# First-batch attention weights turned by TensorE, second-stage scores as one float32 product, and a new order of the work

## The chip, the cores and the metric

One NeuronCore of a Trainium2 chip runs the whole kernel. The metric is the device time of one execution in microseconds (us); each kernel has a median of several runs. The engines are named as the profile names them: PE is TensorE (PEld its weight loads), DVE is VectorE, ACT is ScalarE, POOL is GpSimd, and SP is the engine that issues nearly all DMAs.

## The reference, cut to what matters

Two stages, for 8 batches of 576 positions. The first is attention with a threshold over 8 heads of width 64; the second is a mixture of 4 causal attention experts of width 64, of which each position uses two.

```python
scores = q @ k.T / 8                                  # (8, 8, 576, 576)
thresh = max(scores, -1) - tau
attn = softmax(where(scores >= thresh, scores, -1e9))
x = merge_heads(attn @ v)                             # (8, 576, 512)
logits = x @ w_gate                                   # two of four experts, softmax over the two
for e in range(4):
    a = softmax(causal((x @ wq[e]) @ (x @ wk[e]).T / 8))
    out += gate[e] * (a @ (x @ wv[e]) @ wo[e])        # (8, 576, 512)
```

All inputs and outputs are float32.

## The kernel before

**First stage.** The heads are taken in pairs: a batch has 4 pairs, so there are 32, numbered n. `prep` (L868) loads k, q and v of a pair, turns k and q on PE by products with an identity (L638, shown as L1253) and copies the result to `kx` and `qx` on ACT. The queries of a pair come in tiles of 128; the 64 left over of two pairs share a fifth tile, which the odd pair handles: 9 tiles for two pairs, 18 for a batch. `scores` (L921) does a tile for both heads: four float32 products; two DVE reductions (`copied_min`, L722) that copy the scores from PSUM to a buffer `pp` and keep the minimum of the negated scores; a POOL operation that adds tau; on ACT the threshold (`kinked`, L741) and the exponential with its sum (L737). The weights are then divided by their sum and split into two float16 parts, a high part by POOL (L691) and the rest by DVE (L714), both in `hl` (L949, L950). `turned` (L963) has one DMA transpose on SP's queue put the tile's 18 blocks of 128x128 into `T`. `attnv` (L971) multiplies them with v, which `values_in` (L843) has also split in two float16 parts, after finding its largest value (a DVE reduction, two tiny products with ones, a reciprocal): 5 blocks x 3 terms x 2 heads = 30 products. ACT and DVE write the result as a rounded part and a rest in `x`.

**Second stage.** `moe` (L1193) follows each batch's fourth pair. For each of two expert pairs `projected` (L1015) makes q and k: 12 products for each half of the columns, ACT copies the rounded part from PSUM, and DVE subtracts it to leave the rest (`minus`, L676, shown as L674), so `q2` holds two parts. `scores2` (L1099) makes the scores in three terms (high x high, high x rest, rest x high); then come a masked minimum on DVE (L720), the exponential on ACT, the gate on POOL, `transp2` (turning on PE, copies on ACT, `blocks_out` L953), `attnv2` (float32 products) and `output`.

**Order.** No engine order is written out. Each operation gets a planned cost in ns and a place: the pair's number plus a value of its unit from the table `PLACE` plus one of its engine and output from `PLACE_OP`. `arrange` (L298) runs the whole program through a list schedule with these as priorities, and the order that comes out is each engine's. Even pairs and odd pairs have two sets of places (prefix none or `o`); `attnv2` borrows those of the first stage one to three pairs later (`AV2_AT`). A planned DMA transpose takes 3300 ns of SP and lands after 7000 (`TURN`). `fill` (L488) puts dummy products with `still` (L1250) in PE's long gaps of the first 160 us, so that PE keeps working.

Of the kernel before, what the change touches and what calls it, by code (L numbers as in the profile page):

```python
# [29 lines left out]
TURN = 3300, 7000  # L30
PLACE = {
# [27 lines left out]
    "ot40": 1.234288, "otload": -2.15, "ovload": 6.842465, "ovx": -0.4765129, "ovy": 0.19182, "perm": 3.2453,  # L59
# [4 lines left out]
}  # L64
PLACE_OP = {
    "ACT gw": -56.45884, "ACT kx": 19.09358, "ACT lg": -1.697393, "ACT p2": -0.2764889, "ACT pp": 7.008259,
    "ACT pt2": -3.430901, "ACT q2": 61.64586, "ACT q2d0": -19.44223, "ACT q2d1": -62.4638, "ACT qi": -6.081787,
    "ACT qx": -40.40309, "ACT qz0": -45.39163, "ACT qz1": -1.596204, "ACT tau_t": -6.23236, "ACT tq": -4.485027,
    "ACT v2": -31.44942, "ACT warm": -2.488699, "ACT wkh": -18.97201, "ACT woh": -17.61192, "ACT wqh": -32.6847,
    "ACT wvh": -29.69152, "ACT x": -20.71576, "ACT z0": 6.489924, "ACT z1": 39.36308, "ACT zt": 44.04483,  # L70
    "DVE col": -0.501858, "DVE gate": -41.56914, "DVE gt": -13.63018, "DVE gw": -58.71909, "DVE hl": 0.2197733,
    "DVE lg": -0.01591195, "DVE p2": 0.1799851, "DVE pp": 0.07334633, "DVE q2": 11.57007, "DVE qsc": -9.096009,
    "DVE st": 51.91258, "DVE still": 14.04606, "DVE tau_p": -1.901486, "DVE v2": -1.374655, "DVE vh": -18.09807,
    "DVE warm": -35.69132, "DVE x": -0.4135823, "DVE z0": 2.44509, "DVE z1": 25.41215, "DVE zt": 30.31674,
    "POOL col": -9.007673, "POOL hl": 23.92377, "POOL ident": -28.71514, "POOL mask": 29.11687,
    "POOL mask2": 1.757008, "POOL ones": 0.3521134, "POOL p2": -39.45817, "POOL q2d0": 16.35419,
    "POOL q2d1": -49.53155, "POOL qz0": -10.19174, "POOL qz1": -15.39161, "POOL st": -7.958867, "POOL tie": 30.51963,
    "POOL vh": -26.85869, "POOL vz0": -7.771182, "POOL vz1": -17.71229, "POOL wkl": -19.05416, "POOL wol": 14.28486,
    "POOL wql": 38.65369, "POOL wvh": -23.34791, "POOL wvl": -33.78734, "SP T": -0.2487632, "SP ki": -5.091671,
    "SP lg": -2.212828, "SP out": -56.49631, "SP qi": 6.936229, "SP st": -49.13195, "SP tk": 7.588376,  # L80
    "SP tq": -17.13129, "SP vz0": -2.828946, "SP vz1": 1.694837,
}
# [460 lines left out]
def kernel(  # L543
# [58 lines left out]
    for name, n in SLOTS.items():  # L602
        family(name, words[name], n)
# [680 lines left out]
```

## Time and profile before

| what | us |
|---|---|
| median of 3 runs | 849.94 |
| lowest and highest run | 848.79, 850.33 |
| profiled execution, its own time | 849.39 |
| profiled execution, span from first to last instruction | 847.6 |

The profile's page gives each engine's busy time as a share of the span: PE 92%, PEld 76%, DVE 89%, ACT 80%, POOL 52%. Busy time of PE is modelled, because products overlap in the array, so a busy PE is not one at its peak. The mean granted clock of TensorE is 0.977 of full speed.

### The profile page before, as it was taken

How to read it: one execution, taken by the hardware profiler on the slowest of the kernel's cores; microseconds unless marked ns; L12 is line 12 of the kernel's file. 1: busy time of each engine (PE TensorE's matmuls, PEld its weight loads, DVE VectorE, ACT ScalarE, POOL GpSimd, SP SyncE). 2: the span in 40 equal slices, each digit the busy share in tenths (PEclk: the TensorE clock that was granted, in tenths of full speed). 3: DMA queues.
4: the chain of work that ended last, by engine and by line, in shares of the span. 5: the costliest groups of instructions: out<-in, count | busy, mean ns of one | idle time of the engine just before them, and what ended most of it. 6: DMA issues, size and time to landing. Idle time of an engine off the chain costs nothing.

```text
span 847.6 us, 27874 instructions
## 1 busy us (share of the span) xinstructions
PE 776.1 (92%) x10836; PEld 641.6 (76%) x10836; DVE 752.4 (89%) x2149; ACT 678.5 (80%) x1784; POOL 444.6 (52%) x642
## 2 busy tenths in 40 slices
PE   8989898989999899989999899988999989998898
PEld 5767687767877687767977678776887769776797
DVE  3999989999899889999899998998989998999575
ACT  4887769988689876998689886898869986799464
POOL 5786535566256553566356653565625655366211
PEclk9999999999999899999999999998999999999999
DMA  7999985899758998799956989589966879557602
GB/s 159 187 182 188 184 161 112 161 178 189 141 112 167 156 190 157 109 176 177 177 124 134 189 157 180 110 166 167 179 149 105 168 153 187 140 109 117 135 13 76
DMA packets 442820, 127.65 MB, mean 151 GB/s; under 512 B 429504, under 2 KB 437952, under 8 KB 442688
## 3 DMA queue, kind: packets, MB, share of 16 engines
q1 hardware_dynamic: 440960, 125.48, 78.6%
q8 instruction: 85, 1.39, 0.7%
q10 hardware_dynamic: 1728, 0.39, 0.3%
q14 instruction: 47, 0.39, 0.2%
HBM read 31.47 MB, written 9.44 MB: 48 GB/s over the span
## 4 chain that ended last, share of the span: by engine, by line
DVE 40%; PE 37%; issue 8%; ACT 7%; DMA 5%; POOL 3%; ACTq 0%; SPq 0%; POOLq 0%; DVEq 0%
PE banks L629 33%; DVE hl L714 14%; DVE pp L725 11%; DMA T<-hl 4%; DVE p L720 3%; DVE x L714 2%; DVE vh L714 2%; PE banks L1253 2%; POOL hl L691 2%; DVE col L691 2%; ACT pp L743 2%; DVE col L699 1%; ACT pp L737 1%; ACT p L737 1%; PE banks L1250 1%
## 5 line engine op out<-in xcount | busy, mean ns | idle before, releaser
L691 POOL TENSOR_SCALAR hl<-pp,col 128x576 f16<-128x576 f32 x288 | 233.8, 819 | 138.2 <-DVE col L703 50.7
L714 DVE SCALAR_TENSOR_TENSOR hl<-pp,col,hl 128x576 f16<-128x576 f32 x288 | 269.4, 947 | 18.7 <-POOL hl L691 17.0
L743 ACT ACTIVATE pp<-pp,col 128x576 f32<-128x576 f32 x288 | 212.1, 778 | 29.9 <-POOL col L691 29.1
L725 DVE TENSOR_SCALAR_CACHE_REDUCE pp<-banks 128x576 f32<-128x576 f32 x288 | 211.2, 746 | 12.7 <-PE banks L629 12.5
L737 ACT ACTIVATE pp<-pp 128x576 f32<-128x576 f32 x288 | 194.9, 682 | 0.3
L629 PE MATMUL banks<-kx,qx 64*128 64x288 f32 x1024 | 169.2, 435 | 9.5 <-DVE pp L725 5.6
L629 PE MATMUL banks<-T,vh 128*64 128x128 f16 (+1 forms) x4800 | 145.7, 223 | 21.4 <-DVE pp L725 16.2
L629 PEld LDWEIGHTS <-vh 128*64 128x64 f16 x4800 | 135.2, 116 | 38.6 <-issue 36.6
L691 POOL TENSOR_SCALAR col<-col,tau_p 128x2 f32<-128x2 f32 x144 | 64.6, 449 | 168.7 <-DVE pp L725 76.3
L629 PEld LDWEIGHTS banks<-kx,qx 64*128 64x128 f32 x1024 | 101.1, 192 | 41.1 <-DVE pp L725 12.0
L737 ACT ACTIVATE p<-p,col 128x512 f32<-128x512 f32 (+3 forms) x135 | 79.4, 592 | 51.9 <-DVE col L720 51.2
L691 POOL TENSOR_SCALAR p<-p,col,gw 128x512 f32<-128x512 f32 (+3 forms) x115 | 85.2, 748 | 61.8 <-DVE col L703 45.1
L629 PE MATMUL banks<-wvh,x 128*128 128x260 f32 x320 | 65.3, 289 | 6.9 <-DVE x L714 5.2
L720 DVE CUSTOM_DVE_ANT_0 p<-banks,mask 128x512 f32<-128x512 f32 (+3 forms) x135 | 66.5, 513 | 1.2 <-PE banks L629 1.0
L629 PEld LDWEIGHTS banks<-wvh,x 128*128 128x128 f32 x320 | 51.8, 188 | 9.3 <-DVE x L714 6.4
L663 ACT ACTIVATE pt<-banks 128x384 f32<-128x384 f32 (+2 forms) x128 | 56.5, 511 | 2.6 <-PE banks L1253 1.7
L737 ACT ACTIVATION_READ_ACCUMULATOR pp<-pp 128x1 f32 x288 | 57.4, 199 | 0.0
L629 PE MATMUL banks<-pt,v 128*64 128x128 f32 (+1 forms) x960 | 52.4, 260 | 4.1 <-ACT pt L663 4.1
L714 DVE SCALAR_TENSOR_TENSOR x<-banks,col,x 128x256 fp32r<-128x256 f32 (+1 forms) x96 | 37.3, 407 | 20.1 <-ACT x L661 19.2
L629 PE MATMUL banks<-q,q 64*128 64x256 f32 (+3 forms) x384 | 50.2, 354 | 4.8 <-DVE pp L725 4.1
L629 PE MATMUL banks<-x,wqh 128*128 128x288 f32 x256 | 53.3, 300 | 0.0
L629 PE MATMUL banks<-x,wkh 128*128 128x288 f32 x256 | 53.1, 300 | 0.0
(121 smaller groups left out, 1403.3 us busy)
## 6 DMA issues: line engine op xcount, KB each, us to landing
ki<-in_k_dram SPq DMA_DIRECT2D x32, 256.0 KB, 3.7
vz<-in_v_dram SPq DMA_DIRECT2D x32, 256.0 KB, 3.2
qi<-in_q_dram SPq DMA_DIRECT2D x62, 128.0 KB, 3.1
out_dram<-st SPq DMA_DIRECT2D x29, 256.0 KB, 2.3
T<-hl SPq DMA_TRANSPOSE x144, 5.1
tk<-in_k_dram SPq DMA_DIRECT2D x16, 128.0 KB, 3.4
out_dram<-st SPq DMA_DIRECT2D x10, 128.0 KB, 2.4
vz<-in_v_dram SPq DMA_DIRECT2D x64, 16.0 KB, 2.7
```

Source lines behind the costliest of these rows:

```text
L629: lambda o, x, y: nc.tensor.matmul(o, x, y, start=start, stop=stop))
L663: run(e, t, [dst], [src], lambda d, s: nc.scalar.activation(d, s, AF.Copy))
L691: return m.tensor_scalar(d, s, x_, y_, op0=op0, op1=op1)
L699: lambda d, s: nc.vector.tensor_reduce(d, s, axis=axis, op=op, **({"negate": True} if negate else {}), **({"apply_absolute_value": True} i ...
L714: return nc.vector.scalar_tensor_tensor(d, a_, x_, r.pop(0), op0=op0, op1=op1, **kw)
L720: lambda o, a, i, m: nc.vector.tensor_tensor_reduce(o, i, m, 1.0, 3e38, ALU.add, ALU.min, a))
L725: lambda o, a, i: nc.vector.tensor_scalar(o, i, 1.0, None, op0=ALU.mult, op1=ALU.min, accum_out=a))
L737: return nc.scalar.activation(d, s, AF.Exp, scale=scale, **kw)
L743: lambda d, s, x: nc.scalar.activation(d, s, AF.Prelu, bias=x, scale=-1.0, alpha=1e36))
L1250: nc.tensor.matmul(banks[:, n, :256], still_[:, :P], still_[:, :1].to_broadcast([P, 256]), start=True, stop=True)
L1253: o.fn(*(r.place() for r in (*o.outs, *o.ins)))
```

## The change

1. For the first four pairs (`FIRST = 4`, the first batch) the weights stay float32. POOL alone divides them, in place. `transp` turns a tile's 8 full blocks on PE, and DVE copies them from PSUM; the 64 columns left over are turned for two or three tiles together, and ACT copies those. `attnv32` multiplies in float32 with v as loaded, 5 blocks x 2 heads = 10 products a tile. For these pairs `hl`, the DMA transposes and the whole preparation of v fall away. The new buffers `pa` and `pb` lie in those of `pt2` and `p2`.
2. The second stage keeps q and k as one float32 array: no subtraction on DVE, and the scores are one float32 product for each former three.
3. Each of the four pairs of a batch has its own set of places (prefix none, `o`, `c`, `d`), `attnv2` has its own places, and all places were set anew. Planned costs of float16 products, of one DVE form and of the DMA transpose's landing (7000 to 5300 ns) are changed; these steer the order alone.

```diff
-TURN = 3300, 7000
+TURN = 3300, 5300
+FIRST = 4
...
-AV2_AT = (((1, "av0"), (1, "av1")), ((2, "av1"), (3, "av1")))
...
-             "p2": 2 * SM, "hl": 2 * S, "T": 2 * S, "tk": DM, "tq": DM, "x": S, "v2": (R + 1) * E * D, "q2": 2 * S,
+             "p2": 2 * SM, "hl": 2 * S, "T": 2 * S, "tk": DM, "tq": DM, "x": S, "v2": (R + 1) * E * D, "q2": S,
...
+    for name, x in (("pa", "pt2"), ("pb", "p2")):
+        plan.family(name, plan.families[x])
...
-            t, more = max(62, w * 0.417 + 2), 145
+            t, more = max(31.6, w * 0.417 + 1.6), 145
...
-    q2ds = [const(f"q2d{i}", [P, 2, P], F32R) for i in range(2)]
+    q2ds = [const(f"q2d{i}", [P, P]) for i in range(2)]
...
-        plan.place = (n, name if n % 2 == 0 else "o" + name)
+        plan.place = (n, ("", "o", "c", "d")[n % NPAIR] + name)
...
+        if n < FIRST:
+            return vi[:, :2 * R * D].rearrange("p (h r d) -> p h r d", h=2, r=R), vi[:, 2 * R * D:].rearrange("p (h d) -> p h d", h=2)
         unit(n, "vx")
...
+        if n < FIRST:
+            inverse(ss)
+            unit(n, f"n{s}")
+            for h in range(nj):
+                p = pp[:, h * S:(h + 1) * S]
+                scaled("POOL", p, p, ss[:, h:h + 1], 0.0, ALU.mult, ALU.add)
+            return pp
...
+    def transp(n, s, pp):
+        unit(n, f"f{s}")
+        cols = [j * (S + ST) + c * P for j in range(2) for c in range(R)]
+        return blocks_out([(pp[:, o:o + P],) * 2 for o in cols], plan.tile("pa", [P, 2 * SM], F32), "DVE")
+
+    def attnv32(tiles, pairs, pt, ptt):
...
+                for c in range(R):
+                    for j in range(2):
+                        x = pt[s][:, (j * R + c) * P:(j * R + c + 1) * P][:, sub]
+                        matmul(gs[heads[j]], vm[:, j, c], x, c == 0, False)
+                for j in range(2):
+                    matmul(gs[heads[j]], vt[:, j], at[:, sub], False, True)
...
+        for a, b, c, d, (xh, xl) in parts:
+            copy("ACT", xh[:, c:d], g[:, a:b])
+        for a, b, c, d, (xh, xl) in parts:
+            minus("DVE", xl[:, c:d], g[:, a:b], xh[:, c:d].bitcast(F32))
...
-            ts[s] = turned(n, s, pp[s])
+            ts[s] = (transp if n < FIRST else turned)(n, s, pp[s])
...
+                    if n < FIRST:
+                        unit(n, f"tt{k_}")
+                        ptt = blocks_out([(pp[x][:, SM:SM + P],) * 2 for x in tiles], plan.tile("pb", [P, len(tiles) * P], F32))
...
-                    if t is None:
-                        t = plan.tile("q2", [P, 2, S], F32R)
-                    hi, lo = t[:, 0, cols], t[:, 1, cols]
-                    copy("ACT", hi, src)
-                    minus("DVE", lo, src, hi.bitcast(F32))
...
+                copy("ACT", t[:, cols], g[:, :HS])
...
-                    copy("ACT", q2ds[ep][sl, :, j * ST:(j + 1) * ST], t[sl, :, SM:].bitcast(F32))
+                    copy("ACT", q2ds[ep][sl, j * ST:(j + 1) * ST], t[sl, SM:])
...
-            for i, (x, y) in enumerate(HHL):
-                for g, rows in zip(gs, heads):
-                    matmul(g, q2[0][rows, x, t * P:w], q2[1][rows, y, :w], i == 0, i == 2)
+            for g, rows in zip(gs, heads):
+                matmul(g, q2[0][rows, t * P:w], q2[1][rows, :w], True, True)
...
-                for i, (x, y) in enumerate(HHL):
-                    matmul(g[:, hf, :HS], q2ds[ep][:, x], q2[1][:, y, cols], i == 0, i == 2)
+                matmul(g[:, hf, :HS], q2ds[ep], q2[1][:, cols], True, True)
...
-                    at, unit = AV2_AT[ep][k_] if pre == "M" else (0, f"La{ep}{k_}")
-                    plan.place = (base + at, unit)
+                    plan.place = (base, f"{pre}a{ep}{k_}")
```

All values of `PLACE` and `PLACE_OP` change as well; they are left out here.

## Rows read from the trace of the kernel before

**Rows 1.** Busy time by stage; columns: stretch, length, engines' busy us (count), clock, DMA.

```profile
0.00:88.00 88.00, 78.93 (x966) 59.43 (x967) 71.33 (x168) 64.55 (x151) 59.82 (x100) 0.98 0.97 179
...
288.00:388.00 100.00, 92.74 (x1320) 76.19 (x1318) 92.29 (x268) 83.73 (x223) 53.93 (x76) 0.98 0.85 157
...
788.00:848.00 60.00, 53.89 (x694) 49.50 (x694) 35.24 (x122) 30.34 (x93) 7.67 (x11) 0.98 0.29 71
```

**Rows 2.** The page's chain of work that ended last, by engine.

```profile
DVE 40%; PE 37%; issue 8%; ACT 7%; DMA 5%; POOL 3%; ACTq 0%; SPq 0%; POOLq 0%; DVEq 0%
```

**Rows 3.** The same chain in order of time; columns: start us, length us, what.

```profile
336.09 10.75 PE banks L629 x80
...
435.62 10.74 PE banks L629 x79
...
799.98 22.75 PE banks L629 x193
```

**Rows 4.** Groups of DVE instructions from 0 to 88 us: busy, mean ns, idle before.

```profile
L714 DVE SCALAR_TENSOR_TENSOR hl<-pp,col,hl 128x576 f16<-128x576 f32 x31 | 29.9, 985 | 1.2 <-POOL hl L691 1.2
L725 DVE TENSOR_SCALAR_CACHE_REDUCE pp<-banks 128x576 f32<-128x576 f32 x36 | 26.1, 745 | 9.7 <-PE banks L629 9.6
...
L714 DVE SCALAR_TENSOR_TENSOR vh<-vz,col,vh 128x640 f16<-128x640 f32 x4 | 4.6, 1154 | 1.5 <-POOL vh L691 1.5
L699 DVE TENSOR_REDUCE col<-vz 128x1 f32<-128x640 f32 x5 | 4.1, 811 | 0.2 <-DMA vz<-in_v_dram 0.2
```

**Rows 5.** Groups of ACT and of PE instructions in the same 88 us.

```profile
L743 ACT ACTIVATE pp<-pp,col 128x576 f32<-128x576 f32 x34 | 25.0, 769 | 8.5 <-POOL col L691 8.4
...
L1250 PE MATMUL banks<-still 128*128 128x256 bf16 x266 | 36.1, 289 | 3.0 <-DVE pp L725 1.9 <-DVE still L670 1.2
```

**Rows 6.** DMA queue from 20 to 110 us: packets, MB, share of 16 engines.

```profile
q1 hardware_dynamic: 61545, 16.44, 103.4%
```

**Rows 7.** Groups of the whole span, shapes apart.

```profile
L674 DVE TENSOR_TENSOR q<-banks,q 128x288 fp32r<-128x288 f32 x64 | 27.2, 446 | 8.6 <-ACT q L663 8.3
L665 DVE COPY st<-banks 128x512 f32<-128x512 f32 x33 | 22.6, 685 | 1.1 <-PE banks L629 1.1
...
L663 ACT ACTIVATE pt<-banks 128x320 f32<-128x320 f32 x32 | 12.4, 453 | 0.0
```

**Rows 8.** Timeline of PE, second and first stage: start us, length us, what.

```profile
299.76 1.15 PE L629 MATMUL banks<-pt,v 128*64 128x128 f32 x18
...
318.29 0.96 PE L629 MATMUL banks<-q,q2d 128*128 128x288 f32 x6
319.17 1.86 PE L629 MATMUL banks<-T,vh 128*64 128x128 f16 x60
...
321.86 1.13 PE L629 MATMUL banks<-kx,qx 64*128 64x288 f32 x8
...
336.98 0.55 PE L629 MATMUL banks<-q,q 64*128 64x128 f32 x6
...
348.26 1.00 PE L629 MATMUL banks<-q,q 64*128 64x512 f32 x6
...
366.65 0.66 PE L1253 MATMUL banks<-ident,p 64*128 64x64 f32 x16
```

**Rows 9.** Busy time where a batch's projections and values run; columns as in the first group.

```profile
342.00:349.00 7.00, 7.00 (x61) 5.52 (x59) 6.00 (x18) 6.85 (x18) 4.72 (x9) 1.00 0.29 55
402.00:426.00 24.00, 23.43 (x286) 21.08 (x286) 21.02 (x56) 16.10 (x46) 8.38 (x12) 1.00 0.94 178
```

**Rows 10.** The buffer T: what its readers on PE waited for, and its landing.

```profile
  DMA T<-hl: 5.2, 4
...
DMA to landing us min/median/max: 4.5/5.1/7.6
```

**Rows 11.** Busy time and clock (third number from the end) in three short stretches.

```profile
92.00:94.00 2.00, 0.40 (x4) 0.11 (x1) 1.39 (x3) 0.00 (x0) 2.00 (x3) 1.00 1.21 257
...
95.30:98.70 3.40, 3.21 (x92) 3.21 (x93) 3.40 (x11) 2.98 (x8) 2.40 (x4) 0.50 1.15 191
...
832.00:834.00 2.00, 2.00 (x52) 1.75 (x54) 1.49 (x6) 2.00 (x6) 0.00 (x0) 1.00 0.00 0
```

More of the change, by code (lines that the diff above doesn't have):

```diff
@@ L29 @@
          "x": 10, "v2": 1, "q2": 2, "zt": 2, "z0": 2, "z1": 2, "pt2": 4}
-TURN = 3300, 7000
+TURN = 3300, 5300
+FIRST = 4
 PLACE = {
[27 rows of a table removed]
-    "ot40": 1.234288, "otload": -2.15, "ovload": 6.842465, "ovx": -0.4765129, "ovy": 0.19182, "perm": 3.2453,
[4 rows of a table removed]
[27 rows of a table added]
+    "ctload": 21.58207, "ctt0": 0.8933597, "ctt1": 1.299724, "cvload": 25.75243, "cvx": -0.02764193, "cvy": 0.3941093,
[15 rows of a table added]
+    "ott0": 0.7763555, "ott1": 1.170486, "ovload": -14.83629, "ovx": -0.4914198, "ovy": 0.3953797, "perm": 3.2453,
[5 rows of a table added]
 }
 PLACE_OP = {
[L66 to L81, printed above, removed]
@@ new lines @@
+    "ACT zt": 76.83323, "DVE col": -1.366362, "DVE gate": -80.2003, "DVE gt": -8.634005, "DVE gw": -52.63038,
+    "DVE hl": -0.01902341, "DVE lg": 67.63602, "DVE p2": 0.3523751, "DVE pa": -2.007489, "DVE pp": 0.02345616,
+    "DVE qsc": -14.81346, "DVE st": 56.8961, "DVE still": 17.65341, "DVE tau_p": -10.49955, "DVE v2": -102.4144,
+    "DVE vh": 17.27501, "DVE warm": -8.892884, "DVE x": -1.174117, "DVE z0": 33.70987, "DVE z1": 6.471735,
+    "DVE zt": 34.83497, "POOL col": -13.15804, "POOL hl": 0.2618884, "POOL ident": -24.23104, "POOL mask": 111.6934,
@@ new lines @@
+    "POOL mask2": -12.86903, "POOL ones": -4.150345, "POOL p2": -42.90537, "POOL pp": 7.287512,
+    "POOL q2d0": -6.743555, "POOL q2d1": -38.91802, "POOL qz0": -114.463, "POOL qz1": -56.06971, "POOL st": -7.647755,
+    "POOL tie": 15.6467, "POOL vh": -11.72585, "POOL vz0": -73.20838, "POOL vz1": -14.2186, "POOL wkl": -26.51355,
+    "POOL wol": 58.43931, "POOL wql": 18.79501, "POOL wvh": -5.037461, "POOL wvl": -67.06706, "SP T": -11.86897,
+    "SP ki": 4.855483, "SP lg": -5.583299, "SP out": -156.8427, "SP qi": 15.50643, "SP st": -87.75529,
@@ L82 @@
+    "SP tk": -4.31495, "SP tq": -9.137334, "SP vz0": -52.3161, "SP vz1": -9.390403,
 }
@@ L714, in fn @@
             return nc.vector.scalar_tensor_tensor(d, a_, x_, r.pop(0), op0=op0, op1=op1, **kw)
-        run("DVE", cost("DVE", size(dst), True, accum is not None, True) + 45 * kx, [dst] + ([accum] if accum is not None else []), refs, fn)
+        run("DVE", cost("DVE", size(dst), True, accum is not None, True) + 55 * kx, [dst] + ([accum] if accum is not None else []), refs, fn)
     def masked_min(o, s, m, least):
@@ L815, in later @@
         for t in q2ds:
-            memset("POOL", t.bitcast(F32), 0.0)
+            memset("POOL", t, 0.0)
     def load_weights(c):
@@ L961, in blocks_out @@
         return out
+    def transp(n, s, pp):
[3 more added lines that the diff above has]
+    def attnv32(tiles, pairs, pt, ptt):
+        g = gbank()
+        parts, o = [], 0
+        for s in tiles:
+            at = ptt[:, tiles.index(s) * P:(tiles.index(s) + 1) * P]
+            for i, (vm, vt, xs) in enumerate(pairs if s == R else pairs[-1:]):
+                m, sub = (P, slice(0, P)) if s < R else (ST, heads[i])
+                gs = g[:, o:o + m]
+                for c in range(R):
[4 more added lines that the diff above has]
+                    matmul(gs[heads[j]], vt[:, j], at[:, sub], False, True)
+                if s < R and parts and parts[-1][3] == s * P:
+                    parts[-1][1:4:2] = o + m, s * P + m
+                else:
+                    parts.append([o, o + m, s * P, s * P + m, xs])
+                o += m
+        for a, b, c, d, (xh, xl) in parts:
+            copy("ACT", xh[:, c:d], g[:, a:b])
+        for a, b, c, d, (xh, xl) in parts:
+            minus("DVE", xl[:, c:d], g[:, a:b], xh[:, c:d].bitcast(F32))
     def turned(n, s, hl):
@@ L1011, in pair @@
                         XT[b, hp] = [plan.tile("x", [P, S], F32R) for _ in range(2)]
-                    unit(n, f"av{k_}")
-                    attnv(tiles, [(*held[i][1:], XT[b, hp - odd + i]) for i in range(odd + 1)], ts)
-    def projected(b, ep, base, pre, parts):
+                    pairs = [(*held[i][1:], XT[b, hp - odd + i]) for i in range(odd + 1)]
+                    if n < FIRST:
+                        unit(n, f"tt{k_}")
+                        ptt = blocks_out([(pp[x][:, SM:SM + P],) * 2 for x in tiles], plan.tile("pb", [P, len(tiles) * P], F32))
@@ L1016, in projected @@
+                    unit(n, f"{'f' if n < FIRST else 'a'}v{k_}")
+                    if n < FIRST:
+                        attnv32(tiles, pairs, ts, ptt)
+                    else:
+                        attnv(tiles, pairs, ts)
+    def projected(b, ep, base, pre):
         res = []
         for i, (wh, wl) in enumerate(((wqh, wql), (wkh, wkl))):
-            t = None
             es = slice(ep * P, (ep + 1) * P)
-            whole = None
+            t = plan.tile("q2", [P, S], F32)
             for hf in range(2):
@@ L1022, in projected @@
                 cols = slice(hf * HS, (hf + 1) * HS)
-                for at, cs in parts:
-                    plan.place = (base, f"{pre}p{ep}{i}{hf}")
-                    g = gbank()
-                    mm = [(w, c, x) for c in cs for w, x in ((wh, 0), (wh, 1), (wl, 0))]
-                    for n, (w, c, x) in enumerate(mm):
-                        matmul(g[:, :HS], w[:, c, es], XT[b, c][x][:, cols], n == 0, n == len(mm) - 1)
-                    src = g[:, :HS]
-                    if cs[-1] != NC - 1:
-                        if whole is None:
-                            whole = plan.tile("x", [P, S], F32)
-                        copy("ACT", whole[:, cols], src)
-                        continue
-                    if whole is not None:
-                        part = whole[:, cols]
-                        tt("DVE", part, src, part, ALU.add)
-                        src = part
-                    if t is None:
-                        t = plan.tile("q2", [P, 2, S], F32R)
-                    hi, lo = t[:, 0, cols], t[:, 1, cols]
-                    copy("ACT", hi, src)
-                    minus("DVE", lo, src, hi.bitcast(F32))
+                plan.place = (base, f"{pre}p{ep}{i}{hf}")
@@ L1044, in projected @@
+                g = gbank()
+                mm = [(w, c, x) for c in range(NC) for w, x in ((wh, 0), (wh, 1), (wl, 0))]
+                for n, (w, c, x) in enumerate(mm):
+                    matmul(g[:, :HS], w[:, c, es], XT[b, c][x][:, cols], n == 0, n == len(mm) - 1)
+                copy("ACT", t[:, cols], g[:, :HS])
             if i == 0:
                 for j, sl in enumerate(heads):
-                    copy("ACT", q2ds[ep][sl, :, j * ST:(j + 1) * ST], t[sl, :, SM:].bitcast(F32))
+                    copy("ACT", q2ds[ep][sl, j * ST:(j + 1) * ST], t[sl, SM:])
@@ L1203, in moe @@
             if ep:
-                q2[1] = projected(b, 1, base, pre, parts)
+                q2[1] = projected(b, 1, base, pre)
             pts, p2 = {}, {}
```

7 lines of the change are left out of this document (6 added, 1 removed), and 78 rows, old and new, of the table PLACE.

## The prediction

> **What bounds the kernel now.** I first read busy time by stage [rows 1]. The kernel has three stages: the first batch alone, to about 88 us; seven stretches of about 100 us, each holding one batch's first stage beside the second stage of the batch before; and 60 us in which the last batch's second stage runs alone. One of the seven stands in the rows. A middle stretch has PE at 92.7 and DVE at 92.3 of 100, so no single engine is the bound. The chain of waits says the same: DVE holds 40% of it and PE 37% [rows 2]. In order of time the chain alternates, and a piece of PE work of 10.7 us comes back 99.5 us later [rows 3], which is the period. While PE runs a batch's projections and values it is the bound: in 402 to 426 it is busy for 23.4 of 24 us and DVE for 21.0 [rows 9]. Outside such places DVE leads. In the first 88 us DVE has 71.3 us of work, ACT 64.6 and PE 78.9 [rows 1], but 36.1 of PE's are dummy products [rows 5]. There DVE leads and PE has room. The last 60 us are PE's, with 53.9 busy against 35.2 on DVE [rows 1].
>
> **Part 1, the first batch: DVE.** The batch has 18 tiles, so 36 subtractions that make the low half of `hl` go: 36 x 0.985 = 35.5 us [rows 4]. Four subtractions on v go as well (4.6 us), and four reductions over v (4 x 0.811 = 3.2 us) [rows 4]. What comes is two copies of 128x512 from PSUM for each tile. The nearest row is the output's copy at 0.685 [rows 7], so 36 x 0.685 = 24.7 us. The net is 35.5 + 4.6 + 3.2 - 24.7 = 18.6 us off DVE.
>
> **PE.** Each tile needs 16 half transposes for its full blocks and 2 for its rest. Sixteen took 0.66 us [rows 8], so 18 tiles x 18 x 0.041 = 13.4 us. The old 30 float16 products take 0.93 us (60 in 1.86); the new 10 float32 products, two instructions each in the trace, take 20 x 1.15/18 = 1.28 us [rows 8]. That is 0.35 more for each of 18 tiles, 6.3 us; I count the fifth tiles like the others. PE thus gets 19.7 us more, where 36.1 us of dummies lie [rows 5]. I cost it at nothing: the planner drops dummies where real work comes. Without that cover it would be 19.7 us.
>
> **ACT, POOL and the queues.** ACT gets 16 copies of the turned rests, of 128 or 192 columns. A copy of 320 takes 0.453 [rows 7]. So they cost between 0 and 7.2 us, and I take 0.3 each, 4.8 us, inside ACT's 23.4 idle us of the 88 [rows 1]. POOL's 36 divisions stay, in another type; I cost that at nothing, since POOL is busy for only 59.8 of 88 [rows 1]. Eighteen DMA transposes leave SP's queue, which was at 103.4% of 16 engines from 20 to 110 us [rows 6], and loads queued behind them on SP can go sooner. I give that no time of its own, since DVE and ACT come after it.
>
> What the stage gains is not 18.6 us, because ACT is next: 64.6 + 4.8 = 69.4 us of work. The largest wait that ended ACT's idle time there is 8.5 us for POOL's addition of tau [rows 5], which itself follows DVE's reductions. I take **8.5 us** as the gain: that wait goes, and the new copies fit in the rest of ACT's idle time. The ends are 0 (ACT keeps its pace) and 16 (18.6 x 31/36, the share of the subtractions that lies before 88 us).
>
> **Part 2, the second-stage scores.** The 64 subtractions on q and k go: 27.2 us over 8 batches [rows 7], 3.4 a batch. ACT's copies stay. On PE one expert pair's scores took about 4 x (0.55 + 1.00)/2 + 0.96 = 4.1 us, with the two middle sizes taken between the ends [rows 8]. Float32 products of the same form, with 64 rows, are in the trace: four of 288 columns in 1.13 us, or 0.98 ns a column [rows 8]. The new tiles have 2 x (128 + 256 + 384 + 512) = 2560 columns, so 2.5 us. The fifth tile's two products use all 128 rows, for which no row stands: 0.56 us if they cost the same as products with 64 rows, 1.13 if they can't run beside each other as two halves may. I take 1.13, since both use the whole array. That makes 3.6 in place of 4.1, or 0.5 less; I take 0.4, since each length also holds its last product's end. For two expert pairs PE loses 0.8 us a batch. The ends are -2 and +1 a batch.
>
> **Part 3, the order.** No row prices it. The removed subtractions lie partly where PE leads [rows 9], so in the old order they would be worth little; the new order has to move other DVE work there. I take for it that it leaves as much idle time on the two engines together as now: 7.3 + 7.7 = 15.0 us in the stretch [rows 1]. The new work is 92.7 - 0.8 = 91.9 on PE and 92.3 - 3.4 = 88.9 on DVE. From (P - 91.9) + (P - 88.9) = 15.0 follows P = 97.9. Against 100 this is 2.1 us a stretch, and for seven **14.7 us**. The ends: 0 if PE's waits fill the room, 23.8 (7 x 3.4) if DVE sets everything.
>
> **The tail.** It is PE's: 22.75 us of products in one piece from 799.98 [rows 3]. DVE's savings are covered by it, so I take nothing; the ends are -2 and +1.
>
> **Sum.** 847.6 - 8.5 - 14.7 = 824.4 us of span. The profiled execution took 849.39, which is 1.8 more than its span, and the median of the runs is 0.55 above that execution. So I forecast 824.4 + 1.8 + 0.55 = 826.75, rounded to 827 us.
>
> **The rivals.**
>
> *DVE sets it all.* If the new order always has DVE work ready, the first stage gains its 16 us and each stretch 3.4. Then 850 - 16 - 23.8 = 810 us. DVE's 40% of the chain speaks for it [rows 2], PE at 92.7 against it.
>
> *PE keeps its pace.* If the stretches stay at 100 us because the subtractions lie where PE leads [rows 9], only the first batch gains: 850 - 8.5 = 841 us.
>
> *It doesn't do what it says.* If ACT also holds the first batch, the kernel stays within 0.2% of 850, about what a measurement of it can tell from no change: 848.2 to 851.6.
>
> *Slower: PE stops for late transposes.* The new order counts on 5.3 us to a transposed tile's landing in place of 7.0. Landings run from 4.5 to 7.6 with a median of 5.1, and PE's readers of T waited for only 5.2 us in all [rows 10]. If PE reaches a tile's products before the landing, all products behind them on PE wait, then the next scores, and with these DVE. In the seven stretches there are 126 such tiles. The mechanism decides when the mean stop passes 23.2/126 = 0.18 us, which eats the gain; at 0.25 us it costs 31.5 us, giving 827 + 31 = 858 us. For it: the spread of landings. Against: the new figure lies above the median, and the queue is emptier in the first batch.
>
> *Slower: PE's clock in the first batch.* After PE had been busy for 0.4 us of 2, its granted clock stood at 0.50, the lower level of 1.2 GHz, from 95.3 to 98.7; 52 products, nearly all half transposes, went by at 1.00 [rows 11]. The stage has 78.9 - 36.1 + 19.7 = 62.5 us of real PE work. If a large part ran at the lower level, PE would become the bound, from a share of 27% on: 62.5 x 1.27 = 79.5, the stage's new length. At the lower level throughout it would need 125 us. With some 5 us before PE's first real work the stage ends at 130 in place of 88, and the time is 850 + 42 - 14.7 = 877 us. The Trainium skill has a rule that points this way ("TensorE: Matmul & The Clock Gate", Part 4: PE-mode transpose): turning does not count as PE activity the way products do, so the full clock need not engage. By that rule the removed dummies would be missed and the time would lie towards 877; by the row on the 52 it would not. The row covers 2 us after long products, so it doesn't refute the rule, but float32 products lie between the new transposes.
>
> **How the numbers follow.** Chances: forecast 0.52, DVE sets it all 0.17, PE keeps its pace 0.16, no change 0.04, late transposes 0.08, the clock 0.03. The first three give faster 0.85; same is 0.04; slower is 0.11. The forecast's own spread is 817 to 836. The range of 808 to 846 adds the case at 841 with 5 us above it and most of that at 810. It leaves out both slower cases (0.11), no change (0.04) and some 0.05 below 808.
>
> **What would show it.** In the changed profile: no `hl` or `vh` before the fifth pair; 36 copies of about 0.69 us by DVE to the new buffer; DVE's work before 88 us down by some 16 us; the end of the first batch's reductions some 8 us earlier; no subtraction on q; the period at about 98 us with DVE near 89 of it. The forecast is wrong if the period stays at 100 (PE keeps its pace), if PE's waits for T grow well beyond 5.2 us, or if the clock shows 0.5 for long in the first 80 us.

## The result, and the profile after

The changed kernel takes 824.13 us (median of 4 runs, 821.53 to 825.65) against 849.37 for the kernel before in the same comparison. The ratio is 0.9699, with a 95% interval of 0.9667 to 0.9731: 3% faster. The forecast was 827 us in a range of 808 to 846.

The time by stage, for the changed kernel; the stages are cut where the last reduction of the first batch and the last of all begin. Columns as in [rows 1].

```profile
0.00:81.00 81.00, 76.31 (x998) 59.08 (x1000) 52.40 (x147) 64.37 (x162) 45.47 (x95) 0.98 0.45 96
81.00:758.00 677.00, 625.27 (x8977) 512.33 (x8975) 614.36 (x1799) 582.76 (x1541) 389.59 (x530) 0.99 0.82 154
758.00:824.00 66.00, 58.17 (x718) 50.60 (x714) 36.12 (x123) 32.51 (x101) 10.61 (x14) 0.99 0.33 73
```

The middle stage and the last of the kernel before, cut at 88 as in [rows 1], which is 1.1 us behind its first batch's last reduction, for comparison:

```profile
88.00:788.00 700.00, 643.30 (x9179) 532.66 (x9177) 645.84 (x1861) 583.62 (x1541) 377.08 (x532) 0.98 0.82 154
788.00:848.00 60.00, 53.89 (x694) 49.50 (x694) 35.24 (x122) 30.34 (x93) 7.67 (x11) 0.98 0.29 71
```

The reductions themselves give the exact cuts. First the kernel before, first batch and the rest: count, shortest, median and longest in ns, and where the first and the last begin.

```profile
L725 DVE TENSOR_SCALAR_CACHE_REDUCE pp<-banks x36: 729/745/758, 13.8 to 86.9; 128x576 f32<-128x576 f32 x36
L725 DVE TENSOR_SCALAR_CACHE_REDUCE pp<-banks x252: 727/746/759, 89.6 to 787.6; 128x576 f32<-128x576 f32 x126
```

The same for the changed kernel:

```profile
L744 DVE TENSOR_SCALAR_CACHE_REDUCE pp<-banks x36: 730/752/758, 13.2 to 81.0; 128x576 f32<-128x576 f32 x36
L744 DVE TENSOR_SCALAR_CACHE_REDUCE pp<-banks x252: 724/744/759, 84.8 to 758.1; 128x576 f32<-128x576 f32 x126
```

The first batch ends 5.9 us earlier (86.9 to 81.0). The seven stretches from the first batch's last reduction to the last of all take 677.1 in place of 700.7 us: 23.6 less, 96.7 each in place of 100.1. What follows takes 65.7 (823.8 - 758.1) in place of 60.0, so 5.7 us more. Together this is 23.8 us, the difference of the spans.

The mean of 96.7 hides two kinds of stretch. These are the third, fourth and fifth of the changed kernel, each from one batch's last reduction to the next one's; columns as in [rows 1]:

```profile
271.80:367.00 95.20, 88.56 (x1298) 72.67 (x1296) 89.10 (x262) 84.16 (x223) 56.03 (x77) 1.00 0.91 165
367.00:467.80 100.80, 91.36 (x1293) 74.54 (x1293) 88.53 (x259) 83.31 (x221) 57.41 (x78) 0.96 0.86 161
467.80:567.60 99.80, 90.91 (x1298) 74.24 (x1298) 89.38 (x262) 83.78 (x222) 56.07 (x76) 0.98 0.84 158
```

The other four are like the third: five stretches take 95.0 to 95.5 us, and the fourth and fifth take as long as before. In these two the granted clock fell to its lower level of 1.2 GHz from 377.0, 462.3 and 564.7 us, for 3.4 to 6.8 us each, after PE had stood still for 2.3, 2.7 and 3.3 us for a tile in `T`. In the other five it stayed up, but for 0.5 us at the start of the sixth and 2.2 at the end of the seventh. In the kernel before, all seven have such a fall, and they take 99.0 to 101.1 us.

The chain by engine for the changed kernel, in place of [rows 2]:

```profile
PE 47%; DVE 33%; DMA 9%; issue 4%; POOL 3%; ACT 3%; ACTq 0%; POOLq 0%; DVEq 0%
```

PE now leads, at 47% against DVE's 33%. The groups of the first 80 us of the changed kernel, first DVE, then ACT, then PE (busy us, mean ns, idle before):

```profile
L744 DVE TENSOR_SCALAR_CACHE_REDUCE pp<-banks 128x576 f32<-128x576 f32 x34 | 24.6, 752 | 13.8 <-PE banks L648 13.6 <-PE banks L1298 0.2
L684 DVE COPY pt<-banks 128x512 f32<-128x512 f32 x32 | 20.3, 683 | 5.1 <-PE banks L1298 5.0
...
L762 ACT ACTIVATE pp<-pp,col 128x576 f32<-128x576 f32 x33 | 24.1, 768 | 5.3 <-POOL col L710 5.2
L682 ACT ACTIVATE p<-banks 128x128 f32<-128x128 f32 (+1 forms) x14 | 3.3, 289 | 2.9 <-PE banks L1298 2.9
...
L1295 PE MATMUL banks<-still 128*128 128x256 bf16 x138 | 21.5, 304 | 1.2 <-DVE still L689 1.2
L648 PE MATMUL banks<-pt,vz 128*64 128x128 f32 (+1 forms) x226 | 14.3, 268 | 0.0
L1298 PE MATMUL banks<-ident,pp 64*128 64x64 f32 x288 | 13.7, 230 | 0.9 <-DVE pp L744 0.4
L648 PE MATMUL banks<-p,vz 128*64 128x128 f32 (+1 forms) x56 | 5.2, 265 | 0.0
```

There is no group for `hl` or `vh` before 80 us. DVE has its copies at 683 ns, PE its half transposes and float32 products, and the dummies fell from 266 [rows 5] to 138. DMA from 20 to 110 us, where [rows 6] showed 103.4%:

```profile
q1 hardware_dynamic: 23153, 7.11, 36.8%
```

In the second stage the subtraction on q is gone; what remains is ACT's copy and the float32 scores. These are groups of the whole span, shapes apart:

```profile
L648 PE MATMUL banks<-q,q2d 128*128 128x288 f32 x64 | 19.0, 419 | 0.0
...
L682 ACT ACTIVATE q<-banks 128x288 f32<-128x288 f32 x64 | 25.9, 406 | 25.3 <-PE banks L648 25.0
```

And PE's waits for T, in place of [rows 10]: total us, times, longest.

```profile
PE banks L648 <- DMA T<-hl: 20.4, 16, 3.3
```

### The profile page after: what moved, and what is told of

It reads as the page before. It is cut to its first block, busy times and chain, and to the rows that moved or that the text cites. A ratio compares the mean times of both kernels' runs of the same rounds, so it can differ in the third digit from the quotient of the medians.

```text
span 823.8 us, 27452 instructions
## 1 busy us (share of the span) xinstructions
PE 759.7 (92%) x10680; PEld 622.0 (76%) x10680; DVE 702.9 (85%) x2065; ACT 679.6 (82%) x1800; POOL 445.7 (54%) x638
## 4 chain that ended last, share of the span: by engine, by line
PE 47%; DVE 33%; DMA 9%; issue 4%; POOL 3%; ACT 3%; ACTq 0%; POOLq 0%; DVEq 0%
PE banks L648 41%; DVE hl L733 11%; DVE pp L744 9%; DMA T<-hl 8%; PE banks L1298 4%; DVE p L739 3%; PE banks L1295 2%; DVE x L733 1%; ACT pp L762 1%; DVE vh L733 1%; POOL hl L710 1%; DVE st L684 1%; DVE col L722 1%; DVE col L710 1%; DVE col L718 1%
## 5 line engine op out<-in xcount | busy, mean ns | idle before, releaser
L710 POOL TENSOR_SCALAR hl<-pp,col 128x576 f16<-128x576 f32 x252 | 197.7, 794 | 111.4 <-DVE col L722 34.7
L733 DVE SCALAR_TENSOR_TENSOR hl<-pp,col,hl 128x576 f16<-128x576 f32 x252 | 231.2, 935 | 24.8 <-POOL hl L710 22.3
L648 PE MATMUL banks<-kx,qx 64*128 64x288 f32 x1024 | 163.3, 431 | 12.4 <-DVE pp L744 11.5
L648 PEld LDWEIGHTS <-vh 128*64 128x64 f16 x4200 | 112.4, 112 | 39.0 <-issue 35.6
L648 PE MATMUL banks<-T,vh 128*64 128x128 f16 (+1 forms) x4200 | 122.3, 217 | 20.5 <-DMA T<-hl 20.4
L710 POOL TENSOR_SCALAR p<-p,col,gw 128x512 f32<-128x512 f32 (+3 forms) x115 | 91.8, 805 | 46.0 <-DVE col L722 37.7
L756 ACT ACTIVATE p<-p,col 128x128 f32<-128x128 f32 (+3 forms) x135 | 78.1, 582 | 14.1 <-DVE col L739 14.1
L739 DVE CUSTOM_DVE_ANT_0 p<-banks,mask 128x128 f32<-128x128 f32 (+3 forms) x135 | 65.4, 514 | 3.9 <-PE banks L648 2.8
L648 PE MATMUL banks<-q,q 64*128 64x384 f32 (+3 forms) x256 | 48.6, 467 | 11.9 <-DVE pp L744 11.9
L648 PEld LDWEIGHTS banks<-pt,v 128*64 128x64 f32 x960 | 43.6, 137 | 10.1 <-issue 6.6
```

The lines of the kernel that those rows point to most:

```text
L648: lambda o, x, y: nc.tensor.matmul(o, x, y, start=start, stop=stop))
L710: return m.tensor_scalar(d, s, x_, y_, op0=op0, op1=op1)
L733: return nc.vector.scalar_tensor_tensor(d, a_, x_, r.pop(0), op0=op0, op1=op1, **kw)
L739: lambda o, a, i, m: nc.vector.tensor_tensor_reduce(o, i, m, 1.0, 3e38, ALU.add, ALU.min, a))
L756: return nc.scalar.activation(d, s, AF.Exp, scale=scale, **kw)
```

## The experiments

**One part undone, the order laid anew.** Four kernels undo parts 1 and 2 of the change, or make part 2 alone, and let the planner lay the order with the places as they stand.

`order_alone`: parts 1 and 2 undone.

```diff
-FIRST = 4
+FIRST = 0
...
-            t = plan.tile("q2", [P, S], F32)
+            t = plan.tile("q2", [P, 2, S], F32R)
...
-                copy("ACT", t[:, cols], g[:, :HS])
+                copy("ACT", t[:, 0, cols], g[:, :HS])
+                minus("DVE", t[:, 1, cols], g[:, :HS], t[:, 0, cols].bitcast(F32))
...
-            for g, rows in zip(gs, heads):
-                matmul(g, q2[0][rows, t * P:w], q2[1][rows, :w], True, True)
+            for i, (x, y) in enumerate(HHL):
+                for g, rows in zip(gs, heads):
+                    matmul(g, q2[0][rows, x, t * P:w], q2[1][rows, y, :w], i == 0, i == 2)
```

> The changed kernel with parts 1 and 2 undone: no pair takes the float32 path of the first batch, and the second-stage scores are three terms again; the new places and planned costs stay. Theory (the removed work makes room, the order uses it): little by itself, 843 to 850 us, stretches of 99 to 100 us. Rival (the new order is the gain, the removed work is covered): 824 to 834 us.

Measured: 952.76 us, a ratio of 1.1215 (1.1159 to 1.1271) to the kernel before.

`score_alone`: the kernel before, its places and planned costs, with part 2 (the same lines of `projected` and `scores2` the other way round, `FIRST = 0`).

> The kernel before with part 2 alone: one float32 product for the second-stage scores, no subtraction; the old places and planned costs. Theory (the subtractions lie where PE leads, so without a new order their removal is worth little): 846 to 850 us. Rival (DVE sets the stretches, 3.4 us each for seven): 824 to 830 us.

Measured: 983.18 us, ratio 1.1554 (1.1511 to 1.1597).

`turn_dma`: the changed kernel with the one line `FIRST = 0`.

> The changed kernel with part 1 undone: the first batch's weights are split and turned by DMA as in the other batches; part 2 and the new order stay. Theory (the first batch is worth the 6 us by which its last reduction comes earlier, 86.9 to 81.0): 828 to 833 us. Rival (the float32 path of the first batch is worth nothing, its end is hidden): 824 us within 2. Rival (it is worth DVE's whole 18.6 us): 840 to 843 us.

Measured: 854.07 us, ratio 1.0019 (0.9989 to 1.0049).

`three_terms`: the changed kernel with part 2 undone, as in the diff above, and `FIRST = 4`.

> The changed kernel with part 2 undone: q and k of the second stage in two parts, three terms to a score, the subtractions on DVE; part 1 and the new order stay. Theory (the stretches gain their 3.4 us from the removed subtractions): 843 to 849 us with stretches near 100. Rival (the stretches gain from the new order): 824 to 830 us with stretches near 97.

Measured: 916.64 us, ratio 1.0766 (1.0724 to 1.0807).

None of the nine ranges named in these expectations was met, and three of the four times lie far above both kernels. These runs don't measure the parts. When an operation is taken out or put in, the planner comes to another order, with places that were set for another set of operations. In `score_alone` every engine waits more although DVE has less work, 742.6 us for 752.4. The page of that kernel:

```profile
PE 854.3 (87%) x10799; PEld 676.8 (69%) x10799; DVE 742.6 (76%) x2085; ACT 681.8 (70%) x1784; POOL 427.2 (44%) x642
```

DVE is at 76% of 980.7 us. So the parts have to be tried with the order held.

**Work put back or taken out, the order held.** In the next kernels the planner sees what it saw, or an extra of 1 ns, and every engine keeps its sequence apart from the instructions named.

`minus_kept`: the second stage's subtractions come back, into a buffer that nothing reads.

```diff
                 copy("ACT", t[:, cols], g[:, :HS])
+                plan.op("DVE", 1, 1, [spare[:, cols]], [g[:, :HS], t[:, cols]], lambda d, a, b: nc.vector.tensor_tensor(d, a, b, op=ALU.subtract))
```

> The changed kernel with the 64 subtractions of the second stage put back on DVE, into a buffer that nothing reads; the planner counts each as 1 ns, so every engine keeps its order. 27 us more DVE work, 3.4 a stretch. Theory (DVE bounds the stretches, so its relief is the gain): 3 us and more a stretch, 844 to 850 us. Rival (they lie where PE leads and are covered): 824 to 828 us. Half of it, 832 to 838 us, would mean that about half of them are covered.

Measured: 836.2 us, ratio 0.9826 (0.979 to 0.9862); 12.1 us above the changed kernel's median, or 10.8 by the two ratios, which are from different comparisons and leave some 4 us of doubt. The group added, in that kernel's trace:

```profile
L1093 DVE TENSOR_TENSOR spare<-banks,q 128x288 f32<-128x288 f32 x64 | 28.7, 449 | 3.6 <-ACT q L682 3.0
```

Of 28.7 us of DVE work, 12.1 show in the time (42%). The third value that the expectation named, half of it covered, is the one that held. The reductions of this kernel's profiled execution, all of them and the first batch's:

```profile
L744 DVE TENSOR_SCALAR_CACHE_REDUCE pp<-banks x288: 727/746/760, 14.0 to 765.8; 128x576 f32<-128x576 f32 x144
L744 DVE TENSOR_SCALAR_CACHE_REDUCE pp<-banks x36: 732/753/759, 14.0 to 81.8; 128x576 f32<-128x576 f32 x36
```

Its seven stretches take 765.8 - 81.8 = 684.0 us: 6.9 more than in the changed kernel, but 16.7 less than in the kernel before, with the same subtractions on DVE. This execution took 833.77 us, the shortest of its four runs, and the one of the changed kernel 825.57, near the longest of four, so 6.9 is likely too small.

`three_zero`: the three terms on PE, without subtractions.

```diff
-            for g, rows in zip(gs, heads):
-                matmul(g, q2[0][rows, t * P:w], q2[1][rows, :w], True, True)
+            for i in range(3):
+                for g, rows in zip(gs, heads):
+                    matmul(g, (zero if i == 2 else q2[0])[rows, t * P:w], (zero if i == 1 else q2[1])[rows, :w], i == 0, i == 2, 3)
```

> The changed kernel with three rounded products for each second-stage score, as before the change, but without subtractions: the two small terms read a buffer of zeros, so that part of the scores' precision is left out. The planner counts the three as one, so the order stays. Theory (on PE the two forms cost the same within 0.8 us a batch): 822 to 831 us. Rival (the float32 product is the dearer form on PE): 815 to 821 us. Rival (PE's relief is the gain): 836 us and more.

Measured: 823.14 us, ratio 0.9675 (0.9629 to 0.972), the same as the changed kernel. It makes no difference to the time whether a score is three rounded products or one float32 product.

`score_kept`: part 2 in the kernel before, in that kernel's own order. The subtractions and the two small terms are planned and not issued.

```diff
-                    minus("DVE", lo, src, hi.bitcast(F32))
+                    run("DVE", cost("DVE", size(lo), inps(src, hi), slow=True), [lo], [src, hi], lambda *_: None)
...
-                    matmul(g, q2[0][rows, x, t * P:w], q2[1][rows, y, :w], i == 0, i == 2)
+                    matmul(g, q2[0][rows, x, t * P:w], q2[1][rows, y, :w], True, True, int(i == 0))
```

> The kernel before with part 2 alone, and this time in its own order: all operations are planned as before, but the subtractions and the two small terms are not issued and the first term is a float32 product. Theory (in the old order the subtractions are covered by PE for about half): 833 to 842 us. Rival (covered fully, the new order has to free them): 846 to 850 us. Rival (not covered): 824 to 829 us.

Measured: 851.19 us, ratio 1.0005 (0.9978 to 1.0033). The rival held: the old order has no use for the freed time. From its page:

```profile
PE 781.7 (92%) x10676; PEld 629.6 (74%) x10676; DVE 726.8 (86%) x2085; ACT 677.8 (80%) x1784; POOL 447.3 (53%) x642
```

DVE's work fell by 25.6 us, from 752.4 to 726.8, and its idle time grew by 27.1. This kernel and `score_alone` both make part 2 alone; they differ in their order (and in ACT's small copies of the two parts), and by 132 us in time.

`first_dve`: a second copy behind each copy of the first batch's turned weights.

```diff
+    def twice(d, s):
+        nc.vector.tensor_copy(d, s)
+        nc.vector.tensor_copy(spare[:, :size(d)].rearrange("p (n c) -> p n c", c=D), d)
```

> The changed kernel with a second copy behind each of DVE's 36 copies of the first batch's turned weights, into a buffer that nothing reads, the order kept: 17 to 25 us more DVE work before 81 us, about what part 1 took off DVE. Theory (DVE is busy for 52 of 81 us there and no longer leads, so most is covered): 824 to 831 us. Rival (the relief of DVE is what the first batch gains): 836 us and more.

Measured: 838.14 us, ratio 0.9841 (0.9802 to 0.988); 14.0 us above the changed kernel's median, or 12.1 by the ratios, again with some 4 us of doubt. The added group and the first batch's reductions in its trace:

```profile
L985 DVE COPY spare<-pt 128x512 f32<-128x512 f32 x32 | 15.0, 470 | 1.1
...
L744 DVE TENSOR_SCALAR_CACHE_REDUCE pp<-banks x36: 734/752/758, 13.3 to 94.0; 128x576 f32<-128x576 f32 x36
```

The theory fell. The first batch's last reduction comes at 94.0 in place of 81.0, 13 us later, for 36 copies of 0.47 us (16.9 us), although DVE was busy for only 52.4 of those 81 us. Its busy share there did not say what its work is worth. The 13 us are not all DVE's, though. The same execution from 50 to 80 us:

```profile
50.00:80.00 30.00, 26.50 (x355) 20.68 (x355) 24.23 (x68) 22.97 (x58) 14.04 (x25) 0.89 0.31 70
```

Here the clock fell to its lower level for 6.8 us from 59.8, which it does not in the changed kernel, so up to 3.4 us can be PE's.

`both_back`: the extra work of `minus_kept` and of `first_dve` together.

> The changed kernel with both additions of the earlier runs at once: the 64 subtractions of the second stage and the 36 second copies of the first batch, all on DVE and read by nothing, every engine in the new order. Theory (the gain is DVE's removed work, carried by an order that has PE's work ready; the two shares of 12 and 14 us add up): 847 to 853 us, the time of the kernel before. Rival (the new order, on its own, is worth 8 us or more with DVE's work as before): 835 to 842 us.

Measured: 851.09 us, ratio 0.9998 (0.9977 to 1.0019): the kernel before's time, 27.0 us above the changed kernel where the two single additions gave 12.1 + 14.0 = 26.1 (by the ratios 25.4 and 10.8 + 12.1 = 22.9). Its two added groups:

```profile
L1102 DVE TENSOR_TENSOR lost<-banks,q 128x288 f32<-128x288 f32 x64 | 28.7, 449 | 3.6 <-ACT q L682 2.9
L986 DVE COPY spare<-pt 128x512 f32<-128x512 f32 x36 | 16.6, 460 | 1.2
```

With 45.3 us of work back on DVE, of the 49.5 that the change took off it (752.4 to 702.9), nothing is left of the gain in the whole time, in the new order and with the first batch turned on PE. By stage it is another matter. The profiled execution, cut where the first batch's last reduction and the last of all begin:

```profile
0.00:94.40 94.40, 83.45 (x1027) 62.75 (x1029) 65.32 (x179) 66.11 (x164) 46.51 (x95) 0.95 0.39 85
94.40:781.90 687.50, 635.47 (x8925) 516.51 (x8923) 635.45 (x1861) 584.13 (x1538) 386.71 (x530) 0.99 0.80 152
781.90:851.40 69.50, 62.17 (x738) 54.65 (x732) 39.74 (x131) 32.55 (x101) 10.56 (x14) 0.93 0.32 70
```

The kernel before took 86.9, 700.7 and 60.0. So 13.2 of the 23.6 us gained in the stretches stay with the work put back, and a first batch 7.5 us longer than before and a tail 9.5 us longer use them up. That the two kernels take the same time is a sum of unlike stages.

**The clock and the dummies.** The changed kernel's mean granted clock is 0.988 against 0.977. Before, PE stood still for some 2 us ahead of the same products on transposed tiles in nearly every batch (16.2 us in eight stops, behind a DVE reduction), and the clock fell after it. Two kernels put 24 dummy products ahead of ten such groups:

```diff
+                if o.e == "PE" and o.ins[0].v.fams[0] == "vh":
+                    if turned_at in WARM:
+                        (_, bank), = o.outs[0].v.slot.units
+                        for _ in range(24):
+                            nc.tensor.matmul(banks[:, bank, 384:], still_[:, :P], still_[:, :1].to_broadcast([P, 128]), start=True, stop=True)
+                    turned_at += 1
```

`after_warm`, on the changed kernel:

> The changed kernel with 24 dummy products of 128 columns put ahead of each of ten of its 140 groups of products on transposed tiles, those before which PE stood still for 0.75 us or more in the profiles of this order; nothing else moves. Theory (a stop of over 2 us before such a group is followed by 3.4 us or more at half clock, and each of these costs 3 to 5 us): two to four falls of the clock fewer, 812 to 820 us. Rival (the falls cost nothing, since DVE and ACT are behind them): 822 to 826 us. Rival (the dummies delay PE where the tile is there in time): 827 us and more.

Measured: 823.72 us, ratio 0.9681 (0.9654 to 0.9709), the same as without them. From its waits:

```profile
PE banks L649 <- DMA T<-hl: 6.0, 6, 1.9
```

PE's stops for T went from 20.4 to 6.0 us, filled with dummies, and the time is in the rival's range. But the falls had moved and not gone: between 20 and 800 us there are four in each kernel's profiled execution, 17.1 us at the lower level in the changed kernel and 13.7 here, for a mean clock of 0.988 and 0.990. So the run shows that the dummies are harmless, and not that a fall costs nothing.

`before_warm`, on the kernel before:

> The kernel before with the same dummies ahead of ten groups on transposed tiles, one in nearly every batch, before which PE stood still for 1 to 3 us. Theory (the fall of the clock that follows each of these cost 1.7 us of PE work and more, so part of the change's gain comes from fewer falls): five falls or more go, 834 to 843 us. Rival (the falls are covered there, and the gain is the removed work and the order alone): 847 to 851 us.

Measured: 859.86 us, ratio 1.0095 (1.0063 to 1.0126). This doesn't answer its question. The dummies write to the bank of the group behind them, and there they waited for the same DVE reduction:

```profile
PE banks L1259 <- DVE pp L726: 15.3, 7, 2.4
```

So the stops stayed, the dummies came behind them, and the clock of the profiled execution was no higher (0.978).

`fill_none`: the changed kernel with no dummies after 20 us.

```diff
-    idle = plan.fill(1250.0, 160000.0, 9000.0, 110.0, 217.0)
+    idle = plan.fill(1250.0, 20000.0, 9000.0, 110.0, 217.0)
```

> The changed kernel without dummy products after 20 us (127 fewer). Theory (PE's own work in the first batch, turning included, is dense enough for the full clock): at most two falls more before 100 us, 823 to 830 us. Rival (turning and waiting let the clock fall again and again there): five falls or more before 100 us, 833 us and more.

Measured: 825.87 us, ratio 0.9703 (0.9673 to 0.9733). The theory held. The first batch in that kernel:

```profile
13.00:80.00 67.00, 59.65 (x861) 47.09 (x859) 51.23 (x141) 58.65 (x150) 38.91 (x69) 1.00 0.38 84
```

PE's own work fills 59.65 of 67 us and the granted clock stays at 1.00, the upper level of 2.4 GHz, with no dummy to help. Two falls that the changed kernel does not have come behind it, from 87.2 and 128.1 us, the first of them before 100 us.

## Why the prediction was right, and where not

The time came out 3 us from the forecast, with the sign as forecast and less work on DVE in a new order as the cause, but by terms that missed in both directions. That they add up so well is luck.

**Part 1, DVE.** The work taken off was as worked out. DVE's busy time in the first stage went from 71.3 us in 88 [rows 1] to 52.4 in 81, 18.9 less where some 16 were forecast before 88 us and 18.6 in all; the stretches are of unequal length, so this is a rough match. The copies took 683 ns for 685. On PE, 288 of the 324 half transposes took 13.7 us up to 80 us, for 13.4 forecast for all. ACT's copies of the rests took 289 ns for 0.3 us.

**"I take 8.5 us as the gain".** The term was too large: the last reduction came 5.9 us earlier. The step that failed is "ACT is next". The wait on POOL's addition of tau did not go; it fell from 8.5 [rows 5] to 5.3 us. The chain of waits of the changed kernel from 20 to 81 us names the next bound:

```profile
by line: PE banks L648 48.8%; PE banks L1298 17.1%; PE banks L1295 11.9%; DVE pt L684 8.0%; DVE pp L744 7.4%; POOL pp L710 2.5%; issue 1.8%; DVE col L709 1.1%; DVE x L693 1.0%; POOL wvl L693 0.3%; POOL col L710 0.2%; DVE col L722 0.1%; DVEq
```

PE's products on float32 data, those of scores and those on the weights, hold 48.8% of it, turning (of k, q and the weights) 17.1% and the dummies 11.9%. I had costed PE's 19.7 us at nothing because dummies lay there. They are a cover for PE's time, but a tile's turning and its products also lie in a row between DVE's work and the next free buffer, and dummies don't make that row shorter. `fill_none` shows the other side: without the dummies' 11.9% the time is no better, so they stood where PE waited. And `first_dve` shows that DVE's work is still in that row, with 10 to 13 of 16.9 us passed on. A rough account, argued and not run, is that DVE's relief was worth about that, and PE's longer row took half of it back. The prediction also gave the transposes that leave SP's queue no time of their own. The chain of the kernel before from 20 to 88 us has them:

```profile
by line: DVE hl L714 25.0%; DVE pp L725 21.8%; DMA T<-hl 17.6%; issue 8.8%; PE banks L1250 8.6%; DVE col L691 7.5%; PE banks L629 3.6%; DVE vh L714 3.2%; DVE x L714 2.8%; POOL hl L691 2.2%; DVE col L699 1.5%; DVE col L703 1.3%; PE banks L12
```

How much of the 5.9 us comes from this 17.6%, which is 0 in the changed kernel, no run shows.

**Part 2 and the tail.** "For two expert pairs PE loses 0.8 us a batch" did not come about. The score products before, of the four full tiles and of the fifth, and the four full tiles' now (the fifth's stand above):

```profile
L629 PE MATMUL banks<-q,q 64*128 64x256 f32 (+3 forms) x384 | 50.2, 354 | 4.8 <-DVE pp L725 4.1 <-ACT p L737 0.7
L629 PE MATMUL banks<-q,q2d 128*128 128x288 f32 x96 | 16.1, 303 | 0.0
...
L648 PE MATMUL banks<-q,q 64*128 64x384 f32 (+3 forms) x256 | 48.6, 467 | 11.9 <-DVE pp L744 11.9
```

They took 66.3 us before and take 67.6 now. The term that was too small is the four full tiles: 48.6 us for 16 expert pairs are 3.0 each, where 2.5 was taken from the first stage's products. The fifth tile's product was the dear one, as I had taken it: 19.0/16 = 1.19 us for 1.13. `three_zero` says the same of the time. DVE's 3.4 us a batch did go.

**Part 3, P = 97.9.** Measured 96.7, so the stretches gave 23.6 us for a forecast 14.7. The assumption of equal idle time held: PE and DVE together stood idle for (700 - 643.3) + (700 - 645.8) = 110.9 us over the seven stretches before, and (677 - 625.3) + (677 - 614.4) = 114.3 after, which is 15.8 and 16.3 a stretch. With DVE's load changed in the same order it stayed near, at 14.5 in `minus_kept` and 14.9 in `both_back`; in the old order with less work it rose, to 17.7 in `score_kept` (188 to 388 us). So the rule needs a new order that is as good as the old one, which the prediction assumed. The step that missed is the work put into the equation. PE's busy time fell by 18.0 us over the stretches, 2.6 each, where 0.8 was forecast, and DVE's by 31.5, 4.5 each, where 3.4 was. One source of PE's fall can be read off. A clock of 0.988 for 0.977 means some 0.023 x 847.6 - 0.012 x 823.8 = 9.6 us less PE time lost at the lower level over the whole run, and the prediction had no term for it. Products of the first batch on T that had come after 88 us (6.0 us) are no longer there, but 6.3 us of its float32 products and 1.5 us of its turning now come after 81, so they are no source; the rest stays open. Of DVE's extra 7.7 us, five of the first batch's 36 subtractions of 0.985 us lay after 88 us [rows 4], 4.9 us, but four of the new copies, 2.6 us, come in their place; three more subtractions of the last batch, 2.8 us, now come after the stretches. The gain is also not spread as the equation has it: all of it lies in the five stretches in which the clock stayed up.

**The order.** Part 2 in the old order is worth nothing (`score_kept`, 1.0005), and in the whole time the new order with nearly DVE's old load is worth nothing either (`both_back`, 0.9998); part 1 in the old order was not tried. Together, the changes give the 25 us. In the stretches alone it is otherwise: there 13 to 17 of the 23.6 us stay when DVE's subtractions are put back (`both_back`, `minus_kept`), so they belong to the new order, its fewer falls of the clock included, or to part 1.

**The tail.** Forecast 0, between -2 and +1; it came to +5.7 us. PE's busy time there rose from 53.9 to 58.2, so the new order leaves more for the end. It seems to go with the order: from the last reduction on, `minus_kept`, with the subtractions back, takes 66.2 us, and `score_kept`, without them in the old order, 61.6. This was the term outside its bounds, and no run was made for it. Errors of +2.6, -8.9 and +5.7 us nearly cancelled, which leaves the span 0.6 us from its forecast. The other 2 us of the 3 are the step from a profiled execution to the median, taken as +0.55 us from the kernel before and -1.44 here.

**The rivals.** *DVE sets it all* comes nearer in the stretches, 23.8 us for 23.6, than my 14.7, but not by its mechanism: of the subtractions put back, 42% shows in the time, and of the copies put back in the first batch some 60 to 80%. *PE keeps its pace* is what part 2 did in the old order. *Late transposes* came about in part: PE's waits for T rose from 5.2 to 20.4 us, which is 20.4/126 = 0.16 us a tile, just under the 0.18 that I gave as the deciding point. The waits lie unevenly, and in two of the seven stretches the rival came about: the fourth and fifth, with 5.4 and 3.5 us of waits for T and a fall of the clock behind the longest, gain nothing. The sixth waits 3.1 us, has no fall and takes 95.5 us, which speaks for the fall as the dear part; one stretch does not show it. `after_warm` can't tell how much such stops cost, since dummies fill a stop and don't shorten it. *PE's clock in the first batch* did not happen: the clock stayed at 1.00 from 13 to 80 us even without dummies, with the batch's half transposes in that time (288 up to 80 us in the changed kernel). The rule of the Trainium skill ("TensorE: Matmul & The Clock Gate", Part 4: PE-mode transpose) thus gave the wrong side here. It speaks of turning itself, and here float32 products stood between the turns, so no run here shows turning alone.

**What stays open.** How much of the 25 us is the higher clock. In the changed kernel a stretch with a fall takes about 5 us longer than one without, and falls follow PE's stops, so a good part may hang on them. But the clock alone does not make the gain: with DVE's work back, the ten runs of `both_back` had a clock of 0.978 to 0.992, six of them 0.984 or more, against 0.971 to 0.981 in the 13 runs of the kernel before beside them, and took the same time. No run took the falls away and left the rest. Whether part 1 would gain more with a shorter row on PE was not tried, and neither was the tail.

## What to carry to other kernels

Where a planner or a search has set the order, undo a part with the order held, for instance with the planned cost kept and the instruction left out or put back: an order laid anew moved the time by up to 132 us here and hid parts worth 12 and 14. Removing work from one of two engines that share the bound can be worth nothing in the old order, as part 2 was here, and an order is worth trying with and without the removed work. Compare such runs stage by stage: two kernels of the same time had stages up to 13 us apart. Where a new step gets free time on an engine, look also at whether it lies in the row from buffer to buffer; a busy share of 65% did not mean that DVE had room.

## What was not expected of the hardware

In the same comparison as `after_warm`, 11 runs of the kernel before lay between 848.01 and 854.08 us, and the shortest had the highest granted clock (0.981) and the longest the lowest (0.971). The two move together; which causes which is not shown.

A copy of 128x512 in SBUF took DVE 427 ns in `first_dve` (median; the mean of those up to 95 us is 470, the longest 707), and from PSUM a mean of 683 ns in the changed kernel.
